# First four chunks of a gated-attention and experts kernel: result written straight into x, other order of the first loads

## Chip, cores and metric

The kernel runs on one core of a Trainium2 chip. The metric is the device time of one execution in microseconds (us), as the median of several runs. Engines: PE (TensorE matmul), PEld (its weight loads), DVE (VectorE), ACT (ScalarE), POOL (GpSimd), SP (SyncE, which issues most DMAs). SPq and ACTq are DMA issues on the queues of SP and ACT.

## The reference

Three stages, all float32. A gated linear attention over 4 batches, 8 heads, 768 steps and 48 dims; then a mixture of 4 experts over 3072 tokens of 384; then a block with a product of two projections.

```python
f = 1.0 / (1.0 + np.exp(-f_logit))
for t in range(S):
    state = f[:, :, t, :, None] * state + np.einsum('bhd,bhe->bhde', k[:, :, t], v[:, :, t])
    y[:, :, t] = np.einsum('bhd,bhde->bhe', q[:, :, t], state)
...
p = domain_probs / (domain_probs.sum(-1, keepdims=True) + 1e-09)
for e in range(E):
    h = np.maximum(x @ w1[e], 0.0)
    out += p[:, e:e + 1] * (h @ w2[e])
...
return ((x @ w1) * (x @ w2) @ w3) @ w_out
```

## The kernel before

**Attention in chunks.** Tokens go in 24 chunks of 128; six make a batch. Heads go in four pairs, on 112 partitions: 0 to 47 for the first head of a pair, 64 to 111 for the second. One chunk m passes these steps: a_exp, a_add (f to 1 + exp(-f)), a_scan (running product), a_ln, a_rec (its reciprocal through ACT), a_k (k times the product, on DVE for m < 2, else on POOL; also copies the last column to pends on POOL), a_t, a_q1, a_q2 (q times the refined reciprocal; a_q1 on DVE for m < 2, else POOL; small pw on DVE and pwe on POOL), a_p (transposed k through ACT, scores on PE, masks on DVE into asb), a_y (state times q and asb times v into bank "y", and the new products u into bank "u"), a_x (high part of y by an ACT copy, low part by a DVE subtraction, into yr), a_s (state: DVE sum, POOL product), a_d (eight DMAs that carry yr into the x tile: the 112-partition layout of heads to the 128-partition layout of x). Chunks 0 and 1 take the halves of the head pairs apart (G0, G1) and have PSUM banks of ps_y (one buffer each: y0, y1, y2); later chunks use the three banks of ps_a, where "y" shares a bank with the first head's scores. The tile kT also serves as us.

**Experts.** From attention come blocks of x of 512 tokens (tile xt[b], high and low part). A unit is 128 of 1024 hidden columns of one expert and one block: stage1 is nine matmuls (three passes over high and low parts of weights and x, three pieces of 128 rows) into hps, then ACT and DVE split the relu into hid high and low; stage2 is nine matmuls into three banks y. The first expert's first block goes in two halves of 256 tokens: units 0 to 7 need chunks 0 and 1, units 8 to 15 chunks 2 and 3, then come units of 512. Weights arrive in chunks of 384 KB (load_chunk on SP), and feed() splits them into high (ACT) and low (POOL) parts.

**Order.** Every engine works in the order in which the code issues to it (manual_schedule). The prologue (asteps up to K0 = 2 chunks) is written out by hand; the later steps have due times (the list due) and are spread over the units by time. In the unit loop stage1(i) comes ahead of a part of the plan's steps, then stage2(i - 1), then the rest. warm(n) are matmuls without use between steps. gate() and gate_rows() make the experts' weights from probs.

**Loads.** load_f brings f of two chunks (SP; the first time rows 64 to 111 on ACT's queue), load_kq k and q of two chunks at once, load_v one chunk of v. In the code the first f, k and q (two chunks), probs, v of chunks 0 and 1, three weight chunks, k and q of chunks 2 and 3 and v of chunk 2 are issued ahead of the attention steps; f of chunks 2 and 3 follows once chunk 1's scans have freed its tile. Chunks 0 and 1 issue a_d on ACT's queue, later ones on SP's.

Of the kernel before, what the change touches and what calls it, by code (L numbers as in the profile page):

```python
# [24 lines left out]
def gated_linear_attention_moe_kernel(  # L25
# [65 lines left out]
    state = const.tile([RP, NP, 2, 64], F32, name="state")  # L91
# [9 lines left out]
    def setup():  # L101
# [11 lines left out]
        nc.vector.memset(state[:, :, :, D:], 0.0)  # L113
# [245 lines left out]
    def a_s(m):  # L359
# [14 lines left out]

    def a_d(m):
        b, i = divmod(m, CB)
        if b not in xt:
            xt[b] = xp.tile([128, 2, KD, TB], F32R, tag=f"x{XS[b]}", name="x")
        x = xt[b][:, :, :, i * C:(i + 1) * C]
        yr = at.pop((m, "yr"))  # L380
# [45 lines left out]
    def warm(n):  # L426
# [4 lines left out]


# [4 lines left out]
        (a_exp, 0, G0), (a_exp, 0, G1), (a_add, 0, G0), (a_scan, 0, G0), (a_add, 0, G1), (a_ln, 0, G0),  # L437
        (a_scan, 0, G1), (a_rec, 0, G0), (a_ln, 0, G1), (a_exp, 1), (a_rec, 0, G1), (a_k, 0, G0), (a_t, 0, G0),
        (a_q1, 0, G0), (a_q2, 0, G0), (a_k, 0, G1), (a_t, 0, G1), (a_q1, 0, G1), (a_q2, 0, G1),
        (a_add, 1), (a_scan, 1, G0), (a_p, 0), (a_ln, 1, G0), (a_scan, 1, G1), (a_rec, 1, G0), (a_ln, 1, G1),  # L440
        (a_rec, 1, G1), (load_f, 1), (warm, 4), (a_y, 0), (a_x, 0), (a_k, 1, G0), (a_t, 1, G0), (a_q1, 1, G0), (a_q2, 1, G0), (a_s, 0),
        (a_k, 1, G1), (a_t, 1, G1), (a_q1, 1, G1), (a_q2, 1, G1), (a_d, 0), (warm, 4), (a_p, 1), (warm, 4), (a_y, 1),
        (a_x, 1), (a_s, 1), (a_exp, 2), (a_d, 1),
# [619 lines left out]
```

## Time and profile before

| | us |
|---|---|
| median of three runs (1308.15 to 1310.67) | 1308.39 |
| the profiled execution | 1309.47 |
| its span | 1307.7 |
| PE busy in the span | 1267.4 (97%) |
| DVE, ACT, POOL busy | 632.6, 422.6, 530.4 |

The profile is of one execution. Shares over the span hide its beginning: read it by stretches. In the order-of-time view a row gives start, duration, engine, line, operation, tiles and shapes, and in brackets how long the engine had stood before it and what released it. Lines name the kernel before. A TensorE clock of 1.00 is the full granted clock, 0.50 half of it.

```profile
## 2 busy tenths in 40 slices
PE   7589999999999999999999999999999999999998
PEld 7578878888887888787888778788888999999997
DVE  5257534344445655656425776756724233332422
ACT  3233323332232323223132332323223333333431
POOL 1456615463353334535353454636534222223310
PEclk7789999999999999999999999999999999999999
```

### The profile page before, as it was taken

To read this page: it belongs to the slowest core of one execution; us is meant where nothing else is said; L and a number is where in the kernel's file an instruction comes from. 1 tells how busy PE (TensorE), PEld (TensorE's weight loads), DVE (VectorE), ACT (ScalarE), POOL (GpSimd) and SP (SyncE) were. 2 spreads that over 40 slices of the span, in tenths; PEclk is the share of its full clock that TensorE was granted. 3 is DMA by queue.
4 is the path that set the end of the run, shared out by engine and by line. 5 is a ranking of instruction groups with operands and counts; after the bars stand their busy time and mean duration, and the time that the engine had idled before them with its cause. 6 is when DMAs were issued, how large, how long until landed. Compare 5 with 4: busy or idle time off the path is not lost.

```text
span 1307.7 us, 18243 instructions
## 1 busy us (share of the span) xinstructions
PE 1267.4 (97%) x6939; PEld 1097.6 (84%) x6939; DVE 632.6 (48%) x1027; ACT 422.6 (32%) x743; POOL 530.4 (41%) x415
## 2 busy tenths in 40 slices
PE   7589999999999999999999999999999999999998
PEld 7578878888887888787888778788888999999997
DVE  5257534344445655656425776756724233332422
ACT  3233323332232323223132332323223333333431
POOL 1456615463353334535353454636534222223310
PEclk7789999999999999999999999999999999999999
DMA  7464543534256334344144332423324123231301
GB/s 175 126 188 127 151 102 98 164 94 105 87 142 164 114 107 125 123 102 157 33 129 129 99 112 60 131 81 98 97 85 136 50 82 115 80 115 55 116 1 39
DMA packets 109887, 140.31 MB, mean 107 GB/s; under 512 B 10112, under 2 KB 83296, under 8 KB 109792
## 3 DMA queue, kind: packets, MB, share of 16 engines
q1 hardware_dynamic: 107440, 138.04, 36.2%
q10 hardware_dynamic: 2352, 1.03, 0.3%
q8 instruction: 56, 0.92, 0.3%
q14 instruction: 39, 0.32, 0.1%
HBM read 115.39 MB, written 14.20 MB: 99 GB/s over the span
## 4 chain that ended last, share of the span: by engine, by line
PE 86%; DVE 5%; POOL 2%; issue 2%; ACT 1%; DMA 1%; SPq 1%; ACTq 0%; DVEq 0%; POOLq 0%
PE hps L664 42%; PE y L698 35%; PE wps L577 2%; PE ps L314 2%; PE psy L334 2%; PE psy L328 1%; POOL w L175 1%; POOL acc L718 1%; PE psu L345 1%; DVE dexp L496 1%; DVE hid L671 1%; DVE dexp L495 1%; PE psk L306 0%; ACT hid L670 0%; DMA kq<-in_fkq_dram 0%
## 5 line engine op out<-in xcount | busy, mean ns | idle before, releaser
L664 PE MATMUL hps<-x,w 128*128 128x512 f32 (+2 forms) x2952 | 651.5, 368 | 13.9 <-DMA x<-yr 12.5
L664 PEld LDWEIGHTS hps<-x,w 128*128 128x128 f32 x2952 | 534.7, 190 | 89.2 <-issue 10.6
L698 PE MATMUL y<-hid,w 128*128 128x512 f32 (+1 forms) x1800 | 443.6, 390 | 5.1 <-DVE hid L671 3.9
L175 POOL TENSOR_TENSOR w<-raw,w 128x768 fp32r<-128x768 f32 x160 | 302.0, 1889 | 315.0 <-ACT w L174 271.6
L698 PEld LDWEIGHTS y<-hid,w 128*128 128x128 f32 x1800 | 328.3, 189 | 82.1 <-DVE hid L671 7.2
L671 DVE SCALAR_TENSOR_TENSOR hid<-hps,hid 128x512 fp32r<-128x512 f32 (+1 forms) x200 | 133.6, 668 | 388.8 <-ACT hid L670 388.7
L670 ACT ACTIVATE hid<-hps 128x512 fp32r<-128x512 f32 (+1 forms) x200 | 115.5, 578 | 397.9 <-PE hps L664 396.4
L174 ACT ACTIVATE w<-raw 128x768 fp32r<-128x768 f32 x160 | 133.9, 837 | 58.9 <-PE y L698 51.8
L678 DVE TENSOR_TENSOR ab<-hps,a 128x384 f32<-128x384 f32 x64 | 35.6, 557 | 164.0 <-PE hps L664 164.0
L515 POOL TENSOR_TENSOR dman<-dman,dexp 128x384 f32<-128x384 f32 (+1 forms) x46 | 46.1, 1002 | 167.3 <-ACT dman L513 146.1
L698 PE MATMUL y<-w,hid 128*128 128x384 f32 x576 | 110.7, 337 | 0.1
L718 POOL TENSOR_TENSOR acc<-acc,tmp 128x512 f32<-128x512 f32 x54 | 71.9, 1359 | 79.0 <-DVE tmp L717 79.0
L698 PEld LDWEIGHTS y<-w,hid 128*128 128x128 f32 x576 | 100.7, 188 | 0.5 <-DVE hid L680 0.4
L513 ACT ACTIVATE dman<-dman 128x384 f32<-128x384 f32 (+1 forms) x46 | 24.0, 521 | 153.8 <-DVE dman L512 149.0
L679 ACT ACTIVATE hid<-ab 128x384 fp32r<-128x384 f32 x64 | 33.7, 526 | 114.9 <-DVE ab L678 114.9
L677 ACT ACTIVATE a<-hps 128x384 f32<-128x384 f32 x64 | 31.5, 492 | 77.9 <-PE hps L664 77.2
L680 DVE TENSOR_TENSOR hid<-ab,hid 128x384 fp32r<-128x384 f32 x64 | 35.8, 559 | 37.9 <-ACT hid L679 37.9
L370 POOL TENSOR_TENSOR state<-us,pwe 112x384 f32<-112x384 f32 x20 | 17.2, 859 | 77.2 <-DVE us L369 61.5
L717 DVE TENSOR_TENSOR tmp<-y,pb 128x512 f32<-128x512 f32 x54 | 35.5, 685 | 14.7 <-POOL acc L718 14.7
L577 PE MATMUL wps<-uoh,u 128*128 128x384 f32 x192 | 38.0, 339 | 1.4 <-POOL u L563 0.9
L241 DVE TENSOR_TENSOR_SCAN pi<-ft,capt 112x516 f32<-112x516 f32 (+1 forms) x26 | 39.2, 1506 | 0.3
L264 DVE SCALAR_TENSOR_TENSOR pi<-pi,r 112x512 f32<-112x512 f32 (+1 forms) x26 | 28.7, 1104 | 19.2 <-POOL pends L259 18.9
(83 smaller groups left out, 829.7 us busy)
## 6 DMA issues: line engine op xcount, KB each, us to landing
raw<-in_w_dram SPq DMA_DIRECT2D x112, 384.0 KB, 4.0
raw<-in_u_dram SPq DMA_DIRECT2D x27, 384.0 KB, 3.9
vt<-in_vp_dram SPq DMA_DIRECT2D x24, 288.0 KB, 4.0
x<-yr SPq DMA_DIRECT2D x88, 72.0 KB, 2.9
kq<-in_fkq_dram SPq DMA_DIRECT2D x24, 256.0 KB, 4.9
pb<-pdr SPq DMA_DIRECT2D x24, 256.0 KB, 4.7
raw<-u1d SPq DMA_DIRECT2D x16, 384.0 KB, 3.3
raw<-u2d SPq DMA_DIRECT2D x16, 384.0 KB, 3.2
```

What stands on the lines that cost most here:

```text
L174: nc.scalar.activation(out=w[:, 0], in_=raw, func=AF.Copy)
L175: nc.gpsimd.tensor_tensor(out=w[:, 1], in0=raw, in1=w[:, 0].bitcast(F32), op=ALU.subtract)
L241: nc.vector.tensor_tensor_scan(out=pi.rearrange("p n t -> p (n t)"), data0=gates_of(m, g).rearrange("p n t -> p (n t)"), data1=capt[:, g[0 ...
L515: nc.gpsimd.tensor_tensor(out=out, in0=s, in1=t.bitcast(F32), op=ALU.mult)
L577: nc.tensor.matmul(wps[ft], lhsT=w[:, a, i * 128:(i + 1) * 128], rhs=uoh[g // (NF // 2)][:, g % (NF // 2), b], start=(g == 0 and n == 0), ...
L664: nc.tensor.matmul(ps, lhsT=w[:, wl, j, fs], rhs=x[:, xl, j, t0:t1], start=(n == 0), stop=(n == 3 * KD - 1))
L670: nc.scalar.activation(out=h[:, 0], in_=prods[0], func=AF.Relu)
L671: nc.vector.scalar_tensor_tensor(out=h[:, 1], in0=prods[0], scalar=0.0, in1=h[:, 0].bitcast(F32), op0=ALU.max, op1=ALU.subtract)
L678: nc.vector.tensor_tensor(out=ab, in0=prods[1], in1=a, op=ALU.mult)
L680: nc.vector.tensor_tensor(out=h[:, 1], in0=ab, in1=h[:, 0].bitcast(F32), op=ALU.subtract)
L698: nc.tensor.matmul(yps[t], lhsT=lhsT, rhs=rhs, start=(f == f0 and n == 0), stop=(f == f1 and n == 2))
L718: nc.gpsimd.tensor_tensor(out=at_, in0=at_, in1=tmp, op=ALU.add)
```

## The change

For chunks 0 to 3, y is made on 96 partitions without a gap (both heads add into the same rows, with v padded by zeros), and a_xh (ACT) and a_xl (DVE) write the high and low part from PSUM into x: one piece of 96 partitions and three of 32 that go to partitions 96 to 127. a_x and a_d remain for chunks 4 and on. The state tile has the gapless layout for these chunks. a_st, the state's part of a_y, can be issued by itself. The first chunk's f, k and q are loaded alone, rows 0 to 63 by SP's queue and 64 to 111 by ACT's, the second chunk's behind them. a_add is done by ACT for m < 4; a_k and a_q1 by DVE for m < 3. Chunk 2 goes through all of its preparation in the prologue. The gate moves behind the prologue's steps, and one more weight chunk is split ahead of unit 0.

```diff
-    state = const.tile([RP, NP, 2, 64], F32, name="state")
+    state = const.tile([RP, NP, 128], F32, name="state")
...
-    def load_f(i, engines=(nc.sync, nc.sync)):
+    def load_f(i, chunks=(0, 1), engines=(nc.sync, nc.sync)):
         b, s0 = where(2 * i)
-        for (r0, r1, d), eng in zip(ROWS, engines):
-            for c in range(2):
+        for c in chunks:
+            for (r0, r1, d), eng in zip(ROWS, engines):
                 eng.dma_start(
                     out=ft[r0:r1, c, :, 1:],
                     in_=fkq[b, :, d:d + r1 - r0, 0, s0 + c * C:s0 + c * C + C].rearrange("p r t -> r p t"),
                 )
 
-    def load_kq(i):
+    def load_kq(i, chunks=(0, 2), engines=(nc.sync, nc.sync)):
         b, s0 = where(2 * i)
-        t = kqp.tile([RP, 2, NP, 2 * C], F32, tag="kq", name="kq")
+        if i not in kqs:
+            kqs[i] = kqp.tile([RP, 2, NP, 2 * C], F32, tag="kq", name="kq")
+        c0, c1 = (c * C for c in chunks)
         for j in range(2):
-            for r0, r1, d in ROWS:
-                nc.sync.dma_start(
-                    out=t[r0:r1, j],
-                    in_=fkq[b, :, d:d + r1 - r0, 1 + j, s0:s0 + 2 * C].rearrange("p r t -> r p t"),
+            for (r0, r1, d), eng in zip(ROWS, engines):
+                eng.dma_start(
+                    out=kqs[i][r0:r1, j, :, c0:c1],
+                    in_=fkq[b, :, d:d + r1 - r0, 1 + j, s0 + c0:s0 + c1].rearrange("p r t -> r p t"),
                 )
-        kqs[i] = t
...
     def a_add(m, g=ALL):
         f = gates_of(m, g)[:, :, 1:]
-        nc.vector.tensor_scalar(out=f, in0=f, scalar1=BIG, scalar2=1.0, op0=ALU.min, op1=ALU.add)
+        if m < 4:
+            nc.scalar.activation(out=f, in_=f, func=AF.Identity, bias=1.0)
+        else:
+            nc.vector.tensor_scalar(out=f, in0=f, scalar1=BIG, scalar2=1.0, op0=ALU.min, op1=ALU.add)
...
     def a_k(m, g=ALL):
...
-        eng = nc.vector if m < 2 else nc.gpsimd
+        eng = nc.vector if m < 3 else nc.gpsimd
...
     def a_q1(m, g=ALL):
...
-        eng = nc.vector if m < 2 else nc.gpsimd
+        eng = nc.vector if m < 3 else nc.gpsimd
...
+    def state_of(m):
+        if m < 4:
+            return state[:, :, 0:R].rearrange("p n (h d) -> p n h d", h=2)
+        return state.rearrange("p n (h d) -> p n h d", h=2)[:, :, :, 0:D]
+
+    def a_st(m):
+
+        if m < 4:
+            ps = bank(m, "y")[0:R].rearrange("p (n t) -> p n t", n=NP)
+        else:
+            ps = bank(m, "y")[0:RP].rearrange("p (n t) -> p n t", n=NP)
+        at[m, "y"] = ps
+        if first(m):
+            return
+        for p in range(NP):
+            w = state[:, p, 0:R if m < 4 else RP]
+            nc.tensor.matmul(ps[:, p], lhsT=w, rhs=kq_of(m, 1)[:, p], start=p == 0, stop=False)
+
     def a_y(m):
 
-        asb, vt = at.pop((m, "a")), vts.pop(m)
-        ps = bank(m, "y")[0:RP].rearrange("p (n t) -> p n t", n=NP)
-        if not first(m):
-            for p in range(NP):
-                nc.tensor.matmul(
-                    ps[:, p], lhsT=state[:, p].rearrange("p h d -> p (h d)")[:, 0:RP], rhs=kq_of(m, 1)[:, p],
-                    start=p == 0, stop=False,
-                )
+
+        if (m, "y") not in at:
+            a_st(m)
+        ps, asb, vt = at[m, "y"], at.pop((m, "a")), vts.pop(m)
         for p in range(NP):
             for h, (c0, c1) in enumerate(HEADS):
-                nc.tensor.matmul(
-                    ps[c0:c1, p], lhsT=vt[:, p, 2 * h * D:2 * h * D + c1 - c0], rhs=asb[:, h, p],
-                    start=first(m) and p == 0, stop=p == NP - 1,
-                )
-        at[m, "y"] = ps
+                if m < 4:
+                    nc.tensor.matmul(
+                        ps[:, p], lhsT=vt[:, p, h * D:h * D + R], rhs=asb[:, h, p],
+                        start=first(m) and p == h == 0, stop=p == NP - 1 and h == 1,
+                    )
+                else:
+                    nc.tensor.matmul(
+                        ps[c0:c1, p], lhsT=vt[:, p, 2 * h * D:2 * h * D + c1 - c0], rhs=asb[:, h, p],
+                        start=first(m) and p == 0, stop=p == NP - 1,
...
+    def x_of(m):
+        b, i = divmod(m, CB)
+        if b not in xt:
+            xt[b] = xp.tile([128, 2, KD, TB], F32R, tag=f"x{XS[b]}", name="x")
+        return xt[b][:, :, :, i * C:(i + 1) * C]
+
+    def x_parts(m):
+        x, ps = x_of(m), at[m, "y"]
+        return [(x[0:R], ps[:, 0:KD])] + [(x[R:128, :, j], ps[32 * j:32 * j + 32, KD]) for j in range(KD)]
+
+    def a_xh(m):
+
+        for x, y in x_parts(m):
+            nc.scalar.activation(out=x[:, 0], in_=y, func=AF.Copy)
+
+    def a_xl(m):
+        for x, y in x_parts(m):
+            nc.vector.tensor_tensor(out=x[:, 1], in0=y, in1=x[:, 0].bitcast(F32), op=ALU.subtract)
+        at.pop((m, "y"))
...
-        eng = nc.scalar if m < 2 else nc.sync
+        x, yr = x_of(m), at.pop((m, "yr"))
+        eng = nc.sync
...
+    def feed_(n):
+        feed(0, n)
...
+        (a_exp, 0, G0), (a_add, 0, G0), (a_exp, 0, G1), (a_add, 0, G1), (a_scan, 0, G0), (a_ln, 0, G0),
+        (a_scan, 0, G1), (a_rec, 0, G0), (a_ln, 0, G1), (a_rec, 0, G1), (a_k, 0, G0), (a_t, 0, G0), (a_k, 0, G1),
+        (a_q1, 0, G0), (a_q2, 0, G0), (a_t, 0, G1), (a_q1, 0, G1), (a_q2, 0, G1), (a_exp, 1), (a_add, 1),
+        (a_scan, 1, G0), (a_scan, 1, G1), (a_p, 0), (a_ln, 1, G0), (a_rec, 1, G0), (a_ln, 1, G1), (a_rec, 1, G1),
+        (load_f, 1), (load_kq, 1), (load_v, 2), (warm, 5), (a_y, 0), (a_k, 1, G0), (a_t, 1, G0), (a_q1, 1, G0),
+        (a_q2, 1, G0), (a_k, 1, G1), (a_t, 1, G1), (a_q1, 1, G1), (a_q2, 1, G1), (a_xh, 0), (a_s, 0), (warm, 5),
+        (a_p, 1), (a_st, 1), (feed_, 1), (a_xl, 0), (warm, 3), (a_y, 1), (a_exp, 2), (a_add, 2), (a_scan, 2),
+        (a_xh, 1), (a_xl, 1), (feed_, 1), (a_ln, 2), (a_rec, 2), (a_s, 1), (warm, 5), (a_k, 2), (a_t, 2), (a_q1, 2),
+        (a_q2, 2), (feed_, 1),
...
-        due += [(m, (a_p, m)), (m + 0.35, (a_y, m)), (m + 0.45, (a_x, m)), (m + 0.5, (a_s, m)), (m + 0.6, (a_d, m))]
+        due += [(m, (a_p, m)), (m + 0.35, (a_y, m)), (m + 0.5, (a_s, m))]
+        if m < 4:
+            due += [(m + 0.45, (a_xh, m)), (m + 0.46, (a_xl, m))]
+        else:
+            due += [(m + 0.45, (a_x, m)), (m + 0.6, (a_d, m))]
...
-            due.append((max(m - 3 + 0.55, 1), (load_v, m)))
+            due.append((m - 3 + 0.55 if m > 4 else 1, (load_v, m)))
     due.sort(key=lambda d: d[0])
+    PRO = len(asteps)
...
-        load_f(0, (nc.sync, nc.scalar))
-        load_kq(0)
+        both = nc.sync, nc.scalar
+        load_f(0, (0,), both)
+        load_kq(0, (0, 1), both)
+        load_f(0, (1,))
+        load_v(0)
+        load_kq(0, (1, 2))
+        setup()
         pr = gate_load()
-        setup()
-        load_v(0)
+        feed(0, 0)
         load_v(1)
-        feed(0, 0)
-        load_kq(1)
-        load_v(2)
         warm(24)
-        for st in asteps[:steps_to(K0)] + [(warm, 8)]:
+        for st in asteps[:PRO]:
             run(st)
-            if st == (a_p, 1):
-                feed(0, 1)
-            if st == (a_x, 1):
-                gate_rows(pr)
-                feed(0, 1)
-            if st == (a_q2, 1, G1):
-                gate(pr)
+        gate(pr)
+        gate_rows(pr)
         load_gate(0, 0)
```

## Rows read from the trace of the kernel before

**Rows 1.** Stretches: length, busy PE, PEld, DVE, ACT, POOL, clock, DMA share, GB/s.

```profile
45.10:87.10 42.00, 31.91 (x256) 29.91 (x256) 23.24 (x32) 15.14 (x28) 22.95 (x21) 0.83 0.46 123
87.10:110.30 23.20, 22.42 (x197) 21.67 (x196) 15.63 (x20) 10.51 (x20) 13.37 (x10) 0.91 0.71 202
110.30:1307.00 1196.70, 1183.82 (x6281) 1019.62 (x6279) 576.96 (x929) 385.78 (x676) 484.18 (x363) 1.00 0.35 102
```

**Rows 2.** Order of time (start, duration, instruction): first eviction, chunk 3's y, unit 16.

```profile
45.08 0.38 ACT L670 ACTIVATE hid<-hps 128x256 fp32r<-128x256 f32 x1 [4.55 <-PE hps L664]
...
73.64 1.51 PE L328 MATMUL psy<-kq,state 112*112 112x128 f32 x8 [2.65 <-DVE asb L317]
...
110.29 2.24 PE L664 MATMUL hps<-x,w 128*128 128x512 f32 x9
```

**Rows 3.** TensorE's waits, 0 to 120 us: total, times, longest.

```profile
PE hps L664 <- DMA x<-yr: 12.3, 5, 6.5
PE ps L314 <- DVE kq L275: 5.6, 3, 4.2
...
PE psy L328 <- DVE asb L317: 2.7, 1, 2.7
```

**Rows 4.** Order of time, ACT and DVE in the prologue.

```profile
4.17 0.72 ACT L232 ACTIVATE ft<-ft 112x256 f32<-112x256 f32 x2 [0.52 <-DMA ft<-in_fkq_dram]
...
5.86 0.69 DVE L241 TENSOR_TENSOR_SCAN pi<-ft,capt 112x258 f32<-112x258 f32 x1
...
10.04 0.42 DVE L271 TENSOR_TENSOR kq<-kq,r 112x256 f32<-112x256 f32 x1 [1.20 <-DMA kq<-in_fkq_dram]
...
18.63 0.69 DVE L356 TENSOR_TENSOR yr<-psy,yr 112x512 fp32r<-112x512 f32 x1 [2.66 <-ACT yr L355]
...
23.49 0.42 DVE L275 SCALAR_TENSOR_TENSOR kq<-pi,kq 112x256 f32<-112x256 f32 x1
...
39.68 0.84 ACT L174 ACTIVATE w<-raw 128x768 fp32r<-128x768 f32 x1 [7.04 <-DMA x<-yr]
```

**Rows 5.** Groups by line, 0 to 39 us: busy time, mean ns, idle before.

```profile
L175 POOL TENSOR_TENSOR w<-raw,w 128x768 fp32r<-128x768 f32 x2 | 3.6, 1806 | 6.1 <-ACT w L174 6.1
...
L317 DVE TENSOR_TENSOR asb<-ps,cmask 128x512 f32<-128x512 f32 x4 | 2.6, 686 | 0.4 <-PE ps L314 0.4
...
L355 ACT ACTIVATE yr<-psy 112x512 fp32r<-112x512 f32 x2 | 1.2, 597 | 5.8 <-PE psy L334 5.8
...
L142 ACT ACTIVATE pt<-pT 96x128 f32<-96x128 f32 x1 | 0.3, 272 | 0.1
```

**Rows 6.** Groups by line and shape, 120 to 1000 us: the Identity on ACT.

```profile
L513 ACT ACTIVATE dman<-dman 128x384 f32<-128x384 f32 x45 | 23.7, 526 | 151.1 <-DVE dman L512 146.3 <-issue 4.8
```

**Rows 7.** Order of time: a scan alone, and one beside GpSimd.

```profile
46.29 1.23 DVE L241 TENSOR_TENSOR_SCAN pi<-ft,capt 112x516 f32<-112x516 f32 x1
...
68.69 1.02 POOL L370 TENSOR_TENSOR state<-us,pwe 112x384 f32<-112x384 f32 x1
...
69.05 3.53 DVE L241 TENSOR_TENSOR_SCAN pi<-ft,capt 112x516 f32<-112x516 f32 x1
...
69.66 1.83 POOL L175 TENSOR_TENSOR w<-raw,w 128x768 fp32r<-128x768 f32 x1
```

**Rows 8.** Stretches again: during the first loads, and behind a gap of TensorE.

```profile
5.00:6.00 1.00, 1.00 (x7) 1.00 (x7) 0.97 (x3) 0.33 (x1) 0.18 (x1) 1.00 1.10 241
74.00:76.00 2.00, 2.00 (x17) 1.75 (x17) 1.18 (x3) 1.41 (x3) 0.79 (x1) 0.55 0.92 312
```

**Rows 9.** Chain that ended last, in order of time, at full clock.

```profile
66.02 1.07 PE hps L664 x9
...
121.95 1.09 PE ps L314 x16
...
125.30 0.87 PE psy L328 x8
...
126.17 1.02 PE psy L334 x15
```

More of the change, by code (lines that the diff above doesn't have):

```diff
@@ L112, in setup @@
         )
-        nc.vector.memset(state[:, :, :, D:], 0.0)
         nc.vector.memset(hm, 1.0)
@@ L320, in a_p @@
         at[m, "a"] = asb
-    def a_y(m):
-        asb, vt = at.pop((m, "a")), vts.pop(m)
-        ps = bank(m, "y")[0:RP].rearrange("p (n t) -> p n t", n=NP)
-        if not first(m):
-            for p in range(NP):
-                nc.tensor.matmul(
-                    ps[:, p], lhsT=state[:, p].rearrange("p h d -> p (h d)")[:, 0:RP], rhs=kq_of(m, 1)[:, p],
-                    start=p == 0, stop=False,
-                )
+    def state_of(m):
[13 more added lines that the diff above has]
+            nc.tensor.matmul(ps[:, p], lhsT=w, rhs=kq_of(m, 1)[:, p], start=p == 0, stop=False)
+    def a_y(m):
+        if (m, "y") not in at:
+            a_st(m)
+        ps, asb, vt = at[m, "y"], at.pop((m, "a")), vts.pop(m)
         for p in range(NP):
             for h, (c0, c1) in enumerate(HEADS):
-                nc.tensor.matmul(
-                    ps[c0:c1, p], lhsT=vt[:, p, 2 * h * D:2 * h * D + c1 - c0], rhs=asb[:, h, p],
-                    start=first(m) and p == 0, stop=p == NP - 1,
-                )
-        at[m, "y"] = ps
+                if m < 4:
[7 more added lines that the diff above has]
+                        start=first(m) and p == 0, stop=p == NP - 1,
+                    )
         if last(m):
@@ L368, in a_s @@
         else:
-            nc.vector.tensor_tensor(out=us, in0=u2, in1=state[:, :, :, 0:D], op=ALU.add)
+            nc.vector.tensor_tensor(out=us, in0=u2, in1=state_of(m), op=ALU.add)
         nc.gpsimd.tensor_tensor(
-            out=state[:, :, :, 0:D].rearrange("p n h d -> p (n h) d"), in0=us.rearrange("p n h d -> p (n h) d"),
-            in1=pwe[:, m % 3].rearrange("p n h -> p (n h)").unsqueeze(2).to_broadcast([RP, 2 * NP, D]), op=ALU.mult,
+            out=state_of(m + 1), in0=us, in1=pwe[:, m % 3].unsqueeze(3).to_broadcast([RP, NP, 2, D]), op=ALU.mult
         )
     def a_d(m):
[L376 to L380, printed above, removed]
-        eng = nc.scalar if m < 2 else nc.sync
+        x, yr = x_of(m), at.pop((m, "yr"))
+        eng = nc.sync
         for n in range(2):
@@ L436, in gated_linear_attention_moe_kernel @@
     asteps = [
[L437 to L443, printed above, removed]
+        (a_exp, 0, G0), (a_add, 0, G0), (a_exp, 0, G1), (a_add, 0, G1), (a_scan, 0, G0), (a_ln, 0, G0),
[7 more added lines that the diff above has]
+        (a_q2, 2), (feed_, 1),
     ]
@@ L447, in ahead @@
         return min(1.75, 0.95 + 0.2 * (m - 2))
-    due = [(1.99, (attn_done, 1))]
+    due = []
     for m in range(2, NCH):
@@ L453, in gated_linear_attention_moe_kernel @@
         for i, fn in enumerate(chain):
-            if (fn, m) != (a_exp, 2):
+            if m > 2:
                 due.append((m - lead + 0.08 * i, (fn, m)))
-        due += [(m, (a_p, m)), (m + 0.35, (a_y, m)), (m + 0.45, (a_x, m)), (m + 0.5, (a_s, m)), (m + 0.6, (a_d, m))]
+        due += [(m, (a_p, m)), (m + 0.35, (a_y, m)), (m + 0.5, (a_s, m))]
[3 more added lines that the diff above has]
+            due += [(m + 0.45, (a_x, m)), (m + 0.6, (a_d, m))]
         due.append((m + 0.95, (attn_done, m)))
@@ L460, in gated_linear_attention_moe_kernel @@
         if m > 2:
-            due.append((max(m - 3 + 0.55, 1), (load_v, m)))
+            due.append((m - 3 + 0.55 if m > 4 else 1, (load_v, m)))
     due.sort(key=lambda d: d[0])
+    PRO = len(asteps)
     asteps += [st for _, st in due]
     def steps_to(m):
-        return len(asteps) if m == NCH else 1 + asteps.index((a_d, m - 1))
+        if m in (K0, NCH):
+            return PRO if m == K0 else len(asteps)
+        return 1 + asteps.index((a_xl if m <= 4 else a_d, m - 1))
     def run(step):
```

## Prediction

> **What bounds the kernel now.** I first read the table of stretches [rows 1]. From 110.3 us on TensorE is busy for 1183.8 of 1196.7 us at full clock: nothing ahead of it can shorten that part, it can only start earlier. Ahead of it, from 45.1 us, the granted clock averages 0.83 and 0.91 and TensorE still has gaps, so the change has to be judged in the first 110 us. TensorE's own order of time [rows 2] gives the marks: the first half of the first expert unit is done at 45.1 us, when its eviction starts, and unit 16, the first with 512 columns, starts at 110.29; in between unit 8, the first that reads chunks 2 and 3, ends its first half at 87.1, after two waits for x. Then the waits of TensorE [rows 3]: 12.3 us on the DMA of x, 5.6 on the prepared q (4.2 of it at one place, chunk 2's chain, which starts only behind unit 0), 2.7 on the masked scores. Last the prologue's DVE and ACT rows [rows 4]: chunk 0 waits for its k and q, chunk 1's k is multiplied only after the low part of chunk 0's result (18.63), and ACT stands still for 7.04 us ahead of a weight split while its queue issues chunk 1's x transfers.
>
> **Chunk 0.** The exponential of chunk 0 can't start earlier: its f transfer is the first one in both versions. The +1 of a_add moves from DVE to ACT. An Identity of 384 columns takes 0.53 us on ACT [rows 6] and a copy there 0.85 ns a column (512 in 0.60, 128 in 0.27 [rows 5]), so 256 columns take 0.42. Exp, add, exp, add in halves, four of about 0.4 from 4.17 us on [rows 4], end near 5.8, and the second scan ends near 6.55, as now (5.86 + 0.69 [rows 4]). From there DVE needs k. Now 1.38 MB of f, k and q stand ahead of the last q (the second q1 row began at 10.04 on that DMA); with half-width loads it is 0.69 MB, 3 us less at 241 GB/s [rows 8], so q lands near 7.0 and k near 5.9. k is wanted at 6.6 and q at 7.8: the load stops bounding. Eight DVE steps of 0.42 (the q1 row [rows 4]) and their small ones take 3.4 us: chunk 0 is prepared at 9.95, about 2.8 us sooner than now. The scans of chunk 1 (two of 0.69) then fill DVE until 11.3, while TensorE does the scores, and the masks (two of 0.69 [rows 5], a little overlapped) end at 12.6.
>
> **Chunk 1.** a_xl no longer stands ahead of it, so its eight steps follow the masks at once: 12.6 + 3.5 = 16.1, where now the last q2 ends at 23.9 [rows 4]: 7.8 us earlier. Scores end near 17.1, masks near 18.4.
>
> **Moved at no cost, and their covers.** SP's queue now carries chunk 0's halves, f and v, the second halves of k and q, three weight chunks, v of chunk 1, and only then (they stood ahead of v of chunk 2 and beside the weights) f, k and q of chunks 2 and 3. At 241 GB/s for all of it the second halves (1.7 MB in) land at 9 to 10 (traffic starts near 2 us) and are wanted at 12.6; all 4.9 MB have landed by 22 and a_k of chunk 2 comes after 25. Half of load_f(1) waits for chunk 1's scans (11.3), with k, q and v of the next chunks queued behind it: that lies in the same cover of 3 us, and past it chunk 2 is late by the excess. ACT's queue gets two k and q issues (about 0.6 each) and gate_load's behind the table load; the first exp waits 0.52 for its transfer anyway [rows 4], and without that cover the cost is below 0.5. The gate rows go to memory at about 33 and are wanted at the end of unit 7, past 60. The third split goes from unit 0 to the prologue (1.81 on GpSimd, counted below). The +1 of chunks 2 and 3 costs ACT 0.63 each; ACT was busy for 15.1 of 42.0 us there [rows 1].
>
> **What x costs.** Eight DMA issues a chunk go, 32 in all, and their 2 to 3 us of landing. Instead of one ACT copy (0.60 [rows 5]) and one DVE subtraction (0.69 [rows 4]) there are four of each: 384 columns and three of 128. By the two copy rows [rows 5] 384 columns cost 0.49 and 128 cost 0.27, 1.30 in all; on DVE, with 0.69 for 512 and 0.42 for 256 columns [rows 4], 384 cost 0.55 and 128 cost 0.28, 1.4 in all. That is 0.7 more per engine and chunk. No row shows a copy from 32 partitions to other ones: between 0.27 (128 columns) and 0.60 (512 columns) each; I take 0.27.
>
> **The wait that is added.** a_st(1) writes bank y1, whose pool has one buffer, and a_xl(0) still has to read chunk 0 there. On DVE a_xl(0) stands behind the masks of chunk 1: 18.4 + 1.3 = 19.7. TensorE's queue stands from 17.1 to 19.7 at a_st(1); behind it are warm(3), a_y(1) and all else. A gap of 2.65 us ahead of 73.64 was followed by a clock of 0.55 [rows 2, 8]. So a_st, warm(3) and a_y(1) cost 3.2 us at full and 6.5 at half clock (the full-clock rows doubled): 22.9 to 26.2.
>
> **Chunk 2 ahead of the experts.** DVE then does a_xl(1), the state sum (0.55), k, t, q1 and q2 of chunk 2 at 512 columns (0.69 each) and the small ones: 3.4 us, plus 1.5 to 2.5 behind GpSimd's second split (1.81 [rows 5]) and state product (about 0.85), since the end of k's chain waits for pends in that queue. Then the four gate steps, 1.0 us, moved here; gate_rows' transpose stands in TensorE's queue ahead of unit 0 and waits for them. Unit 0 can start at 30 to 35.5; I take 33.4, nearer the half-clock end, because TensorE has stood for over 5 us. Its nine matmuls at half clock take 2.1: it ends at 35.5 against 45.1. **Term 1: 9.6 us (8 to 13).**
>
> **Units 0 to 8.** Full-clock costs from the chain [rows 9]: 1.06 for half a unit, 1.09 for the scores of a_p and about 0.55 for its transposes, 0.87 + 1.02 for a_y and about 0.55 for its u. From the end of unit 0's first half to that of unit 8's TensorE has 15 halves (15.9), two a_p (3.3) and two a_y (4.9), 24.1 us, and about 1.8 for its first microseconds at half clock: 25.9. Now the same stretch is 42.0 [rows 1], with chunk 2's chain (4.2 of waits) and the x transfers in it. What comes next as late: DVE. Chunk 4's add and scan and chunk 3's t still lie in units 2 to 5, beside GpSimd's splits. A scan of 1.23 us lasted 3.53 while a state product and a split ran back to back on GpSimd [rows 7], and the masks behind it held TensorE for 2.65 [rows 2, 3]. Placing the steps in their queues I get: hid behind t in unit 3, 1.1; hid and masks behind chunk 4's scan in units 5 and 6, 2.7; a_xh and a_xl of chunk 3 behind unit 7's eviction, 0.8; loss of clock after them, 1. Together 5.6: 31.5 us. **Term 2: 10.5 us (6 to 16).**
>
> **Units 8 to 16** take 23.2 us now for 20.0 of work, a clock of 0.91 with the start at half, after the x wait [rows 1]. Without that wait: **term 3, 2 us (0 to 2.5).** After that nothing changes: chunks 4 on keep their DMA, and the 0.2 us that unit 32 waits for x stays.
>
> Sum: 9.6 + 10.5 + 2.0 = 22 us. The profiled execution took 1309.47 (span 1307.7 and 1.8 around it); the median of the runs is 1308.39, 1.1 lower. 1309.5 - 22 = 1287.5, and 1286.4 from the median: I say 1287.
>
> **Rivals.**
> 1. The covers hold: the bank wait doesn't drop the clock, DVE gets in between GpSimd's steps, and the stretch takes 26 to 28. For it: chunk 2's work is gone from it, and a scan beside no GpSimd work took 1.23 [rows 7]. Against: GpSimd still has 7 splits. Gain 27 to 30, 1280. Chance 0.17.
> 2. DVE and GpSimd exclude each other in full. GpSimd's 20 us in units 0 to 7 (7 splits of 1.81 [rows 5], k and q1 twice at 1.2, states and small ones) and DVE's scans, adds and products with two SBUF inputs (some 6) would run one after the other, each wait handed on through hid. Price up to 2.3 a collision [rows 7]; with three more than I counted on the path, the gain is 15, 1293. Chance 0.15. The Trainium skill (SBUF — State Buffer, Who interferes with whom) has this rule: DVE with two SBUF inputs contends with GpSimd, and who issues first blocks the other for its whole instruction. The 3.53 us of the scan agree.
> 3. **Slower:** the clock. Waits at a_st(1), at the gate and behind DVE come so close that TensorE does units 0 to 16 at half clock. Work of 24 + 20 us would take 44 more; from 22 us of it at half clock the gain is gone, and at 30 the time is 1316. Against: now, with 12.3 us of DMA waits [rows 3], the mean clock was still 0.83 and 0.91 [rows 1]. Chance 0.03. The Trainium skill (TensorE: Matmul & The Clock Gate, HAM oscillation) describes a kernel that returns to the slow clock after every wait; the 0.55 after 73.64 is such a return.
> 4. The change moves the wait only: chunk 3's x is as late as its DMA was, because y of chunk 3 hangs on the same queues, and term 1 alone is left less its lost clock; 1299. Chance 0.04; that it eats term 1 too and nothing is left, 0.03.
>
> **How the numbers follow.** Forecast 0.58 (1283 to 1291), rival 1 0.17, rival 2 0.15, rival 3 0.03, rival 4 0.04 and its tail 0.03. From 1279, the end of rival 1, to 1297, past rival 2, about 0.87 are covered, and I leave it at that, since the unknown terms are bounded by those ends. A measurement of this kernel tells 0.2% (2.6 us) from no change. Faster 0.94, same 0.03, slower 0.03.
>
> **What would show it.** No x transfers before those of chunk 4; chunk 0 prepared at about 10 and chunk 1 at about 16; a wait of TensorE of 2 to 3 us on the DVE subtraction near 17 to 20; a wait on the gate up to about 33; unit 8's first half done at 67; unit 16 at about 88. Wrong would be: unit 0 after 36, copies to shifted partitions at several times 0.27, a wait on q1 or k left in chunk 0, or a stretch of units 0 to 8 at 36 us or more.

## Result, and the profile after

The changed kernel took 1297.32 us (median of 4 runs, 1296.23 to 1299.17), the kernel before 1309.08 beside it: a ratio of 0.991, 95% interval 0.9893 to 0.9928. Measured a second time, beside its variants, it took 1297.91 (5 runs, 1296.14 to 1299.18), ratio 0.9915, 0.990 to 0.993. It is faster by some 11.5 us, where 22 were forecast: the time lies 6 us above the forecast's 1283 to 1291, and just past 1297, the upper end of what the forecast and its rivals covered.

The profiled execution took 1299.17 us with a span of 1297.4. Its stretches, cut at the marks of [rows 1] (unit 0's first half evicted, unit 8's first half evicted, unit 16 starts); the columns are those of [rows 1]:

```profile
39.36:72.89 33.53, 30.42 (x257) 28.21 (x256) 20.02 (x31) 15.17 (x33) 19.09 (x17) 0.91 0.65 184
72.89:99.43 26.54, 22.52 (x195) 21.87 (x193) 16.65 (x20) 10.64 (x19) 16.73 (x12) 0.87 0.55 160
99.43:1297.00 1197.57, 1183.65 (x6281) 1019.79 (x6279) 574.08 (x930) 385.43 (x675) 481.52 (x361) 1.00 0.35 102
```

Against [rows 1], the part ahead of the first mark shrank from 45.1 to 39.4 us (term 1: 5.7), the second from 42.0 to 33.5 (term 2: 8.5), and the third **grew** from 23.2 to 26.5 (term 3: -3.3). The rest is as long as before, to 1 us. 5.7 + 8.5 - 3.3 = 10.9, and unit 16 starts 10.9 us sooner, at 99.43 instead of 110.29 [rows 2].

TensorE's waits in the first 120 us, as in [rows 3] (total, times, longest):

```profile
PE pT L139 <- DVE praw L134: 8.5, 1, 8.5
PE y L747 <- DVE hid L720: 4.0, 1, 4.0
PE psy L341 <- DVE x L390: 2.8, 1, 2.8
...
PE y L747 <- ACT hid L719: 2.0, 1, 2.0
...
```

The 12.3 us on the x transfers and the 5.6 on q of [rows 3] are gone. New are 8.5 us on the gate values (praw), 2.8 on the low part of x, and 4.0 and 2.0 on hid, a DVE and an ACT result of the expert units. The order of time shows the first two (DVE and PE lines are given in one fence, by engine):

```profile
19.82 1.45 DVE L390 TENSOR_TENSOR x<-psy,x 96x384 fp32r<-96x384 f32 x4
...
27.98 1.46 DVE L390 TENSOR_TENSOR x<-psy,x 96x384 fp32r<-96x384 f32 x4 [5.29 <-ACT x L386]
...
34.39 1.88 DVE L132 TENSOR_SCALAR psum__398<-psum__398 128x24 f32<-128x24 f32 x1
...
21.41 1.78 PE L341 MATMUL psy<-kq,state 112*96 112x128 f32 x8 [2.83 <-DVE x L390]
...
36.96 0.45 PE L139 MATMUL pT<-ident,praw 128*96 128x128 f32 x1 [8.48 <-DVE praw L134]
37.06 2.27 PE L713 MATMUL hps<-x,w 128*128 128x256 f32 x9
```

Chunk 0 is prepared at 10.1 and chunk 1 at 17.0. At 21.41 the state matmul of chunk 1 starts, when bank y1 is read; its eight matmuls take 1.78, at a granted clock of 0.57 from 21.41 to 23.20. Unit 0 stands until 37.06 behind the gate's four steps, which on DVE's queue come after chunk 2's preparation. One of them, on 24 columns, lasts 1.88 us from 34.39, to 36.27. GpSimd ran a weight split beside it, to 36.24 (a row of the view of the chain that ended last):

```profile
34.44 1.80 POOL w L174
```

The 4.0 us on hid are the largest surprise. Order of time at that place, DVE, then GpSimd, then TensorE:

```profile
32.10 0.69 DVE L267 SCALAR_TENSOR_TENSOR pi<-pi,r 112x512 f32<-112x512 f32 x1 [0.85 <-POOL pends L262]
...
82.31 7.12 DVE L267 SCALAR_TENSOR_TENSOR pi<-pi,r 112x512 f32<-112x512 f32 x1
89.35 1.74 DVE L426 TENSOR_REDUCE xsum<-x 128x1 f32<-128x1536 f32 x1
91.02 0.41 DVE L720 SCALAR_TENSOR_TENSOR hid<-hps,hid 128x256 fp32r<-128x256 f32 x1
...
82.22 3.63 POOL L174 TENSOR_TENSOR w<-raw,w 128x768 fp32r<-128x768 f32 x2
85.81 1.30 POOL L274 TENSOR_TENSOR kq<-kq,r 112x512 f32<-112x512 f32 x1
87.06 1.82 POOL L174 TENSOR_TENSOR w<-raw,w 128x768 fp32r<-128x768 f32 x1
...
91.48 2.08 PE L747 MATMUL y<-hid,w 128*128 128x256 f32 x8 [4.02 <-DVE hid L720]
```

Step t of chunk 5 on DVE lasted 7.12 us, while GpSimd ran two weight splits, q1 and a third split without a pause from 82.22 to 88.88; in the prologue the same step (of chunk 2, at 32.10) takes 0.69. Behind t on DVE's queue stood the sum of x and the hid that TensorE waited for. From 90 to 96 the granted clock is 0.50.

The same step of chunks 3 and 4 met GpSimd's queue too, and was through after the first of its instructions:

```profile
51.57 1.76 DVE L267 SCALAR_TENSOR_TENSOR pi<-pi,r 112x512 f32<-112x512 f32 x1 [2.47 <-POOL pends L262]
...
66.09 2.28 DVE L267 SCALAR_TENSOR_TENSOR pi<-pi,r 112x512 f32<-112x512 f32 x1 [1.29 <-POOL pends L262]
...
51.49 1.29 POOL L274 TENSOR_TENSOR kq<-kq,r 112x512 f32<-112x512 f32 x1
...
52.73 2.31 POOL L174 TENSOR_TENSOR w<-raw,w 128x768 fp32r<-128x768 f32 x1
...
66.01 1.81 POOL L174 TENSOR_TENSOR w<-raw,w 128x768 fp32r<-128x768 f32 x1
...
67.78 1.74 POOL L274 TENSOR_TENSOR kq<-kq,r 112x512 f32<-112x512 f32 x1
```

There t ended 0.55 us after the GpSimd instruction that it met, and it was GpSimd's next one that took longer: a split 2.31 instead of 1.82, a q1 1.74 instead of 1.30. At 82.31 t ended 0.55 us after the last of four, and all four kept their times.

### The profile page after: what moved, and what is told of

Same layout as the page of the kernel before. It is cut to its first block, busy times and chain, and to the rows that moved or that the text cites. A ratio compares the mean times of both kernels' runs of the same rounds, so it can differ in the third digit from the quotient of the medians.

```text
span 1297.4 us, 18212 instructions
## 1 busy us (share of the span) xinstructions
PE 1262.4 (97%) x6935; PEld 1094.5 (84%) x6935; DVE 634.1 (49%) x1035; ACT 427.5 (33%) x760; POOL 529.8 (41%) x413
## 4 chain that ended last, share of the span: by engine, by line
PE 88%; DVE 5%; POOL 3%; issue 2%; ACT 1%; DMA 1%; POOLq 0%; DVEq 0%; ACTq 0%
PE hps L713 43%; PE y L747 35%; PE wps L626 2%; PE ps L317 2%; PE psy L357 2%; PE psy L341 1%; POOL w L174 1%; PE warm L467 1%; POOL acc L767 1%; PE psu L367 1%; DMA raw<-in_w_dram 1%; DVE dexp L545 1%; DVE hid L720 1%; DVE pi L267 1%; DVE dexp L544 1%
## 5 line engine op out<-in xcount | busy, mean ns | idle before, releaser
L727 DVE TENSOR_TENSOR ab<-hps,a 128x384 f32<-128x384 f32 x64 | 35.6, 556 | 164.1 <-PE hps L713 164.1
L726 ACT ACTIVATE a<-hps 128x384 f32<-128x384 f32 x64 | 31.5, 492 | 77.5 <-PE hps L713 76.8
L267 DVE SCALAR_TENSOR_TENSOR pi<-pi,r 112x512 f32<-112x512 f32 (+1 forms) x26 | 33.6, 1294 | 14.1 <-POOL pends L262 13.8
L626 PEld LDWEIGHTS wps<-uoh,u 128*128 128x128 f32 x192 | 34.1, 188 | 4.3 <-POOL u L612 1.6
```

The costliest lines, as they stand in the source:

```text
L267: nc.vector.scalar_tensor_tensor(out=pi, in0=pi, scalar=-1.0, in1=r, op0=ALU.mult, op1=ALU.mult)
L626: nc.tensor.matmul(wps[ft], lhsT=w[:, a, i * 128:(i + 1) * 128], rhs=uoh[g // (NF // 2)][:, g % (NF // 2), b], start=(g == 0 and n == 0), ...
L727: nc.vector.tensor_tensor(out=ab, in0=prods[1], in1=a, op=ALU.mult)
```

## Experiments

Theory: three costs keep half of the gain away, one after another, and each has a cause of its own: the one buffer of bank y1, the gate's steps behind chunk 2's preparation (and one of them beside GpSimd), and t beside GpSimd's four instructions. Rival: they cover each other, or what one gives another takes.

What an edit is worth "by the ratios" is counted from 0.9915, the ratio of the changed kernel's second measurement; from 0.991, each mend is worth 0.65 us less and each undoing 0.65 more. The 95% intervals leave each of these figures open by some 3 us, so the traces have to carry the argument.

**Another bank for y of chunk 1.**

```diff
+        if (m, which) == (1, "y"):
+            return ps_a.tile([128, 512], F32, tag="C", name="psy")
         if m < 2 and which in "kyu":
```

> The changed kernel, but y of chunk 1 gets the idle bank C, so that a_st(1) needs not wait for a_xl(0). Theory (the one-buffer bank sets this wait, and the wait drops TensorE's clock): the wait of 2.83 us of the state matmuls on the DVE subtraction is gone or under 0.5, a_st(1) starts near 18.6 instead of 21.41, the clock stays full, u of chunk 1 is done near 23.5 instead of 27.1, unit 0 starts 3 to 4 us earlier than 37.06, and the time falls by 3 to 4 us below that of the changed kernel. Rival (the prologue ends by the DVE and GpSimd queues, not by this wait): a_st(1) moves, but unit 0 starts within 1 us of 37.06 and the time is the same.

Measured: 1293.52 us (1292.53 to 1294.74), ratio to before 0.9888, 0.9868 to 0.9907. TensorE in order of time:

```profile
17.57 1.16 PE L319 MATMUL ps<-kq 48*128 48x128 f32 x16
18.66 1.11 PE L343 MATMUL psy<-kq,state 112*96 112x128 f32 x8
...
32.68 0.42 PE L139 MATMUL pT<-ident,praw 128*96 128x128 f32 x1 [8.58 <-DVE praw L134]
```

The state matmul follows the scores at once and takes 1.11 us instead of 1.78. From chunk 1's scores to unit 0 it takes 15.2 us; in the two profiled executions of the changed kernel it took 19.6 and 18.0. The wait was a cost of its own. By the ratios the edit is worth 0.0027, 3.5 us. Unit 16 starts at 93.09, sooner by 6.3 or 3.5, and not all of that is the wait: here the granted clock was 0.50 until 35.6 us, 2.9 us past unit 0's start, and in the changed kernel until 45.5 and 42.7, 8.5 us past it. The runs don't show why. (The intervals of one mend and of the changed kernel still touch; what settles it is the sum of the three, below.)

**The gate's steps ahead of chunk 1's x.**

```diff
             run(st)
-        gate(pr)
+            if st == (a_scan, 2):
+                gate(pr)
         gate_rows(pr)
```

> The changed kernel, but the four DVE steps of the gate stand right behind chunk 2's scan, where DVE stood idle from 22.7 to 28.0 us, instead of behind chunk 2's preparation. Theory (TensorE's queue is held at the gate's transpose by a DVE queue that has chunk 2's preparation first): TensorE's wait of 8.48 us is gone, the gate's second step takes about 0.2 instead of 1.88 us, unit 0's first matmul starts near 29.5 instead of 37.06, then chunk 2's scores wait for q until about 34.2; unit 1 starts 4 to 5.5 us earlier than 42.0 and the time falls by 4 to 6 us. Rival (x, the weights or DVE's order hold unit 0 just as long): unit 0 starts after 34 and the time falls by under 2 us.

Measured: 1292.95 us (1292.77 to 1293.12), ratio 0.9883, 0.9864 to 0.9902. The gate's step and TensorE:

```profile
22.37 0.18 DVE L132 TENSOR_SCALAR psum__361<-psum__361 128x24 f32<-128x24 f32 x1
...
27.85 1.93 PE L713 MATMUL hps<-x,w 128*128 128x256 f32 x9
...
33.72 2.08 PE L317 MATMUL ps<-kq 48*128 48x128 f32 x16 [2.25 <-DVE kq L278]
```

With GpSimd idle (from 21.1 to 28.4 us) the step takes 0.18 us instead of 1.88. Unit 0 starts at 27.85 and no longer waits for chunk 2's preparation, which stood ahead of the gate on DVE; that chain comes next as late, with 2.25 us at the scores. Worth 4.2 us by the ratios.

**No weight split in two units** (each unit's loop enqueues one; units 12 and 13 now none).

```diff
-            feed(i, 1)
+            feed(i, 0 if i in (12, 13) else 1)
```

> The changed kernel, but no weight chunk is split in units 12 and 13 (the splits come two units later). Theory (DVE's product t of chunk 5, 7.12 us long where it takes 0.69 alone, was kept out by GpSimd's steps that followed one another without a gap): t takes under 3 us, TensorE's wait of 4.02 us on hid near 87 is gone or under 1, the clock there stays full, unit 16 starts 4 to 6 us earlier than 99.43, and the time falls by 4 to 6 us. Rival (t is long for another reason, such as its own wait or the memory, or the weights become late): t stays over 5 us, or a wait for weights takes the place, and the time moves by under 1.5 us.

Measured: 1292.2 us (1291.54 to 1292.75), ratio 0.9875, 0.9853 to 0.9898. The same place, DVE and GpSimd:

```profile
82.52 1.76 DVE L267 SCALAR_TENSOR_TENSOR pi<-pi,r 112x512 f32<-112x512 f32 x1
...
82.44 1.30 POOL L274 TENSOR_TENSOR kq<-kq,r 112x512 f32<-112x512 f32 x1
```

With only q1 beside it (GpSimd's next row starts at 85.59) t lasts 1.76 us and ends 0.5 after q1 does; the wait of 4.0 is gone, and the stretch from unit 8 to unit 16 takes 19.93 us instead of 26.54. Worth 5.2 us by the ratios: the wait and the half clock behind it. In the profiles in which GpSimd's four instructions stood there, t lasted 7.11 or 7.12 (both of the changed kernel; the bank, gate, loads, chunk 2 and both value-matmul edits).

**The narrower value matmuls.** Chunks 0 to 3 now use 96 output columns for each head (16 matmuls take 1.91 us at full clock); the old form has 64 for rows 0 to 63 and 48 for rows 64 to 111, in turn.

```diff
-                if m < 4:
-                    nc.tensor.matmul(
-                        ps[:, p], lhsT=vt[:, p, h * D:h * D + R], rhs=asb[:, h, p],
...
+                nc.tensor.matmul(
+                    ps[c0:c1, p], lhsT=vt[:, p, 2 * h * D:2 * h * D + c1 - c0], rhs=asb[:, h, p],
```

> The changed kernel with the value matmuls of chunks 0 to 3 in the form of before: per pair of heads one of 64 and one of 48 output columns into rows 0 to 63 and 64 to 111, instead of two of 96 columns that add into the same rows. Rows of x are then those of other heads, so its output is not the reference's; the number of instructions is the same, and a clearing of the state tile (0.5 us on idle DVE) is added at the start. Theory (two matmuls of 96 columns follow one another, two of 64 and 48 ran side by side): the 16 records of a chunk take 1.1 us instead of 1.9 at full clock, 0.8 us a chunk, and the time falls by 1.5 to 3.5 us. Rival (the 96 columns cost nothing of their own, the longer time was the clock): 1.9 us stays, and the time with it.

> The old form of the value matmuls of chunks 0 to 3 (64 and 48 columns; rows of x are then other heads'), again on the chip of the changed kernel, since the first time on another chip left open what it is worth. Theory (0.82 us of each chunk's value matmuls are on the path): 2.5 to 3.5 us below the changed kernel. Rival (hidden, or given back by stalls later): within 1 us of it.

Measured: 1296.0 us (1295.42 to 1296.41; ratio 0.9906, 0.9884 to 0.9929), and on the chip of the changed kernel 1296.72 (1296.15 to 1297.02) against its 1297.91 (1296.14 to 1299.18). The matmuls are faster,

```profile
13.46 1.10 PE L352 MATMUL psy<-asb,vt 128*64 128x128 f32 x15
```

but of the 1.5 to 3.5 and the 2.5 to 3.5 us expected 1.2 are left, and the ranges overlap. The stretch from unit 0 to unit 8 was 31.8 us in the first run and 33.2 in the second, against 33.5; two chunks at 0.82 would make 31.9. In both runs the granted clock was lower from 60 to 70 us (0.85 and 0.83, in the changed kernel 1.00), which takes part of the gain back. Whether more than 1.2 us can be had stays open.

**Undoing the direct x.**

```diff
-        if m < 4:
+        if m < 0:
...
-        eng = nc.sync
+        eng = nc.scalar if m < 2 else nc.sync
...
-        (a_q2, 1, G0), (a_k, 1, G1), (a_t, 1, G1), (a_q1, 1, G1), (a_q2, 1, G1), (a_xh, 0), (a_s, 0), (warm, 5),
+        (a_q2, 1, G0), (a_k, 1, G1), (a_t, 1, G1), (a_q1, 1, G1), (a_q2, 1, G1), (a_x, 0), (a_s, 0), (warm, 5),
```

> The changed kernel with the direct write into x undone for chunks 0 to 3: y on 112 partitions, a_x and a_d with eight DMAs a chunk as before (ACT's queue for chunks 0 and 1, SP's for 2 and 3), the state tile in the old layout and cleared once; all else (loads, chunk 2 ahead, order) stays. Theory (the direct write is the larger part of the gain, less what its 96-column matmuls and the bank wait cost): x of chunk 1 lands near 38 to 40, unit 0's bulk starts 1 to 3 us later than 37.06, unit 8 waits 3 to 5 us for x of chunk 3 and the clock falls there, the value matmuls are 0.8 us a chunk shorter; the time rises by 3 to 8 us over the changed kernel. Rival (the order of the steps and chunk 2 ahead carry the gain, the DMAs are hidden behind them): the time is within 2 us of the changed kernel or below it.

Measured: 1307.6 us (10 runs, 1304.52 to 1310.0), ratio 0.9984, 0.997 to 0.9998: some four fifths of the gain are gone, more than expected. ACT's queue (ACTq) and engine, then DVE:

```profile
19.28 0.71 ACTq L422 DMA_DIRECT2D x<-yr  x1
...
20.03 4.79 ACTq L422 DMA_DIRECT2D x<-yr  x3
25.00 3.50 ACTq L424 DMA_DIRECT2D x<-yr  x4
28.55 0.63 ACT L233 ACTIVATE ft<-ft 112x512 f32<-112x512 f32 x1 [8.06 <-DMA x<-yr]
...
29.88 1.23 DVE L245 TENSOR_TENSOR_SCAN pi<-ft,capt 112x516 f32<-112x516 f32 x1 [10.47 <-ACT ft L238]
```

It isn't the landing that costs most. The issues of chunk 0's x stand on ACT's queue until 28.5, so the exponential and the scan of chunk 2 come 8 to 9 us later; chunk 1's eight, from 30.67, stand ahead of ACT's next work until 35.9. The gate's transpose waits 20.6 us, and unit 0 starts at 44.75. So this run prices the transfers together with their place on ACT's queue; what they would cost from SP's queue wasn't tried.

**Undoing the split first loads; undoing chunk 2 ahead of the experts.**

```diff
-        load_f(0, (0,), both)
-        load_kq(0, (0, 1), both)
-        load_f(0, (1,))
+        load_f(0, (0, 1), both)
+        load_kq(0)
```

```diff
-        (a_p, 1), (a_st, 1), (feed_, 1), (a_xl, 0), (warm, 3), (a_y, 1), (a_exp, 2), (a_add, 2), (a_scan, 2),
+        (a_p, 1), (a_st, 1), (feed_, 1), (a_xl, 0), (warm, 3), (a_y, 1), (a_exp, 2),
...
-            if m > 2:
+            if (fn, m) != (a_exp, 2):
```

> The changed kernel with the first loads of before: f of chunks 0 and 1 together, then k and q of both chunks at full width on SP's queue; v of chunk 0 and all else in the order of the changed kernel. Theory (the load set the start of chunk 0's products and everything behind it is a chain): the first q product starts near 10 again instead of 7.96, chunk 0 is prepared near 12.8 instead of 10.1, unit 0 starts 2 to 3 us later than 37.06 and the time rises by 2 to 3 us. Rival (the idle time of DVE and TensorE behind it takes the delay up): unit 0 within 1 us of 37.06, the time the same.

> The changed kernel with chunk 2's preparation behind its exponential back in the units (a_add to a_q2 by their due times, a_k and a_q1 on GpSimd). Theory (it moves a wait rather than removing it: in the prologue it holds unit 0 for 6 us at the gate, in the units it holds chunk 2's scores): unit 0 starts near 31 instead of 37.06, but chunk 2's scores wait for q and start after 41, where they now start at 40.0, and more DVE steps meet GpSimd's splits; the time rises by 1 to 5 us. Rival (the preparation ahead costs more than it gives): the time falls by 2 to 5 us.

Measured: 1300.63 us (1298.37 to 1303.38), ratio 0.9937, 0.9916 to 0.9958; and 1304.17 (1301.62 to 1304.72), ratio 0.9961, 0.9948 to 0.9975. The loads are worth 2.9 us by the ratios: chunk 0 is prepared at 11.9 instead of 10.1. Chunk 2's early preparation is worth 6.0: without it unit 0 starts sooner, at 33.71, but its k is late,

```profile
43.33 1.01 PE L309 MATMUL psk<-ident,kq 112*128 112x112 f32 x4 [2.70 <-POOL kq L261]
46.02 2.08 PE L317 MATMUL ps<-kq 48*128 48x128 f32 x16 [1.68 <-DVE kq L278]
```

and its scores start at 46.02 instead of 40.00. The interval of the loads' run touches that of the changed kernel, so what shows their worth is the trace: unit 0 starts at 40.55 instead of 37.06 or 34.20, and unit 16 at 100.90 instead of 99.43 or 96.56. The other two undoings lie clear of it: as arranged here, the direct x and chunk 2's early preparation pay.

**The three mends together,** once beside other variants and again on the chip of the changed kernel.

> The changed kernel with the three edits of the earlier runs together: bank C for y of chunk 1, the gate behind chunk 2's scan, no splits in units 12 and 13. Theory (the three waits lie one after the other on TensorE's path): unit 0 starts near 25, chunk 2's scores near 30, unit 16 near 82 to 85 instead of 99.43, and the time falls by 12 to 16 us below the changed kernel. Rival (each takes the place of another, so that the gains overlap): unit 16 starts after 88, the time falls by under 9 us.

> The changed kernel itself, beside its own variants on one chip, so that they can be set against it directly. Both theories: 1297 us, ratio 0.991 to before, unit 16 at 99.4.

> The three mends again, on the same chip as the changed kernel and as the fourth edit. Theory (the three costs stand one after another and add up): 16 us below the changed kernel, interval within 0.985 to 0.990 of it. Rival (part of the sum was a difference of chips): under 12 us below it.

Measured: 1281.53 us (1281.16 to 1282.53), ratio 0.9795, 0.9777 to 0.9813; again, 1282.15 (1281.71 to 1282.48) against 1297.91 for the changed kernel on the same chip. That is 15.8 us less, where the single gains make 3.5 + 4.2 + 5.2 = 12.9: within what the intervals leave open they add up, and the rival falls. This kernel beats both. Its stretches between the same marks:

```profile
26.48:61.67 35.19, 29.36 (x256) 27.11 (x255) 23.57 (x35) 15.15 (x33) 22.29 (x21) 0.95 0.63 177
61.67:81.60 19.93, 19.93 (x195) 19.48 (x193) 11.95 (x20) 8.96 (x17) 13.21 (x10) 1.00 0.61 175
```

The second stretch is 1.7 us longer than the changed kernel's 33.53: unit 0 is done so early that the wait for chunk 2's scores (2.25 us) now lies in it. The third stretch is now its work at full clock, 19.93 us. The 26.54 of the changed kernel are these, the wait of 4.0, and 2.6 from the 5.2 us that TensorE then worked at half clock.

**The add of chunks 4 and 5 on ACT,** on top of the three mends.

```diff
-        if m < 4:
+        if m < 6:
             nc.scalar.activation(out=f, in_=f, func=AF.Identity, bias=1.0)
```

> The three mends together (bank, gate, no splits in two units), and besides the addition of 1 in chunks 4 and 5 on ScalarE instead of VectorE. Theory (VectorE's add of chunk 4 lasted 2.79 us from 46.15 because GpSimd was working; ScalarE, which waits behind it for 6.22 us at 50.30, has room): scan at 46.2 instead of 48.98, so the unit's last hid on ScalarE is written at about 49 instead of 51.57, TensorE's wait of 2.0 us there goes and the time is 1.5 to 2 us below the three alone. Rival (the stretch is bound by VectorE's and GpSimd's sum, so what leaves at one place is waited for at the next, here the scan itself lasts 3 us instead of 1.2): within 0.5 us of the three alone.

Measured: 1281.64 us (1280.62 to 1281.83), 0.5 less than the three mends beside it, with ranges that touch. DVE with the three mends, and with this edit:

```profile
46.15 2.79 DVE L239 TENSOR_SCALAR ft<-ft 112x512 f32<-112x512 f32 x1
48.98 1.23 DVE L244 TENSOR_TENSOR_SCAN pi<-ft,capt 112x516 f32<-112x516 f32 x1
```

```profile
46.31 3.60 DVE L244 TENSOR_TENSOR_SCAN pi<-ft,capt 112x516 f32<-112x516 f32 x1
...
46.21 0.83 POOL L414 TENSOR_TENSOR state<-us,pwe 112x384 f32<-112x384 f32 x1 [0.45 <-DVE us L413]
47.00 1.83 POOL L174 TENSOR_TENSOR w<-raw,w 128x768 fp32r<-128x768 f32 x1
```

The rival holds: the add is gone from DVE, and the scan that takes its place beside the state product and the split lasts 3.60 instead of 1.23. TensorE's wait on hid fell from 2.0 to 1.5 only.

## Why the prediction was right in direction and wrong in size

**Chunk 0, chunk 1, x: right.** Chunk 0 was said for 9.95 and came at 10.1, chunk 1 for 16.1 and came at 17.0. No x transfer stands ahead of chunk 4's. Copies to other partitions cost what the rows of straight ones gave: 0.266 us for 128 columns, 0.486 for 384, and 0.287 and 0.549 on DVE (forecast 0.27, 0.49, 0.28, 0.55).

**The added wait: right in place, too small.** Forecast were 2.6 us until 19.7 and half clock after; it was 2.83 until 21.41, since the masks of chunk 1 ended 1.5 us later than said. Its u was done at 27.1, past the forecast range of 22.9 to 26.2. Two costs were missed: the value matmuls at 96 columns, 1.91 us where the sum took 1.02 from the old form [rows 9], and that x of chunk 1 costs its 1.35 on ACT and its 1.46 on DVE one after the other, not side by side. The listed parts of the forecast for unit 0 make 28.8 to 33.1 (22.9 + 3.4 + 1.5 + 1.0 and 26.2 + 3.4 + 2.5 + 1.0), not the 30 to 35.5 that it states: the 1.4 us of a_xl(1), which it names, are not in the 3.4, and what else makes up the difference it doesn't say.

**Term 1, 9.6 forecast, 5.7 measured.** Besides these, the step "the four gate steps, 1.0 us" failed: they took 2.8, because one of them fell beside a GpSimd split. Unit 0 was said for 33.4 and started at 37.06, past the 36 that the prediction named as wrong. The size also varies from one execution to the next: in the second profiled one (1296.14 us) chunk 1's scores started at 16.20 instead of 17.42, its y ran at full clock, unit 0 started at 34.20, and term 1 was 8.6; the other two stretches were the same to 0.01 us. In both, the long wait at the gate was followed by a clock of 0.50 until 42 us or later.

**Term 2, 10.5 forecast, 8.5 measured: nearly right.** The stretch took 33.5 us for 31.5 forecast. Hid waits of 2.0 in unit 6 and 0.7 on x of chunk 3 were foreseen at those places (2.7 and 0.8); the 1.1 behind t in unit 3 did not come. In all TensorE stood for 3.1 us (4.6 forecast) and worked for 30.4 (26.9 forecast, the lower clock included); 1.8 of that come from the two 96-column matmul groups, 1.91 each where the sum took 1.02.

**Term 3, 2 forecast, -3.3 measured: the step that failed.** It was costed as "without that wait", the x wait at its start, and nothing was asked of DVE and GpSimd in units 8 to 16. There t met GpSimd's queue when it ran four instructions without a pause, and the 6.4 us that t lost came out as 4.0 of wait and 2.6 of clock. In the kernel before, the same step of the same chunk stood beside two splits as well, and came between them: t ended 0.55 us after the first split (96.50 to 98.32), and the second, from 98.35 on, took 2.23 us instead of 1.8:

```profile
96.58 2.29 DVE L264 SCALAR_TENSOR_TENSOR pi<-pi,r 112x512 f32<-112x512 f32 x1 [2.39 <-POOL pends L259]
...
96.50 4.08 POOL L175 TENSOR_TENSOR w<-raw,w 128x768 fp32r<-128x768 f32 x2
```

So the meeting was there to be read before; that it would last 7.12 us was not. The edit that takes splits away there shows that they caused the wait. What decides whether DVE gets its turn after one GpSimd instruction or after four stays open: no run here tests it.

**Rival 2 was the mechanism, at another place and price.** It looked for collisions in units 0 to 7 and put one at up to 2.3 us, from one scan [rows 7], with 15 us of gain at worst; the one that counted came between units 8 and 16 and cost 6.4. The Trainium skill (SBUF — State Buffer, Who interferes with whom) says that whoever issues first has the shared ports for its whole instruction. The trace agrees at 51.57 and 66.09, where t waits for the one instruction that had started 0.08 us ahead of it. The 7.12 us show more than that: between four GpSimd instructions standing back to back, DVE got no turn. The scan of [rows 7] was such a case already: it ended at 72.58, 1.1 us after the second GpSimd instruction, not after the first, so its 3.53 us, which the prediction took as agreeing with that sentence, are more than it gives. Rivals 1 and 4 fall by the measured stretches, though rival 4's 1299 lies near the measured time by chance; rival 3's clock losses are there (37 to 45 and 90 to 96 us at 0.50), but never over all units.

## What to carry to other kernels

When waits are taken out of a stretch, its engines run closer, so ask of every DVE step in it what GpSimd then runs beside it, and give a meeting two prices: one GpSimd instruction, and GpSimd's whole unbroken run. In this one kernel the same step paid the first at two places and the second, four instructions, at a third. A step that is moved to a quieter place for one engine can stand behind a long chain on another: four small gate steps held a whole unit. Give a bank that is rewritten early a buffer of its own before counting on the early write.

## What the chip showed that was not expected

- A DVE step on two SBUF inputs took 0.69 us alone, 1.76 and 2.28 where it came in after one GpSimd instruction, and 7.12 where it waited for four in a row; a step on 24 columns took 0.18 alone and 1.88 beside a split. Where DVE came in after one, GpSimd's next instruction took 0.4 to 0.5 us longer; where it waited for four, these kept their times.
- Sixteen value matmuls of 96 output columns take 1.91 us; of 64 and 48 columns, in turn for rows 0 to 63 and 64 to 111, 1.09.
- Eight DMA issues on ACT's queue took from 19.3 to 28.5 us in one place, over 1 us each, and 5.2 us for the next chunk's eight; ACT stood for 8.06 us in the first case before its next work.
